# Transposing two blocks ahead, running half-array tiles in two groups, and loading w1 in two halves (RWKV-5 attention and sentence MoE)

## Chip, cores, metric

One core of one Trainium2 chip. The metric is device time in microseconds (us), lower is better. Runs come with the granted clock of TensorE. Ratios are the mean time of one kernel's fast runs over that of the other's fast runs of the same rounds, so they are not quite the ratio of the medians quoted beside them. A run is called slow when it took over 1.5% more than the fastest run of the same kernel; slow runs stay in the medians and ranges but out of the ratios. In traces PE is TensorE (PEld its weight loads), DVE VectorE, ACT ScalarE, POOL GpSimd.

## The reference

B = 4 sequences of S = 768 tokens, H = 8 heads of D = 48; F = 1024; 8 experts. First a linear attention with decay, then a mixture of experts that picks one expert per whole sequence:

```python
for t in range(S):                       # attention, per batch and head
    cur = (u * k_t) outer v_t
    y[t] = r_t @ (state + cur)
    state = w * state + k_t outer v_t
x = y as [B, S, H * D]
e = argmax(mean over S of x @ w_gate)    # one expert per sequence
out = gate_weight * (relu(x @ w1[e]) @ w2[e])
```

Note what the gate means for time: which expert's w1 and w2 a sequence needs is known only after its last token has been through the attention.

## The kernel before

A sequence is cut into 3 blocks of 256 tokens, 12 blocks g in all (N = 12, NB = 3). For block g: `transposes(g, c)` turn the scaled k and r (full 128*128 array), `scores` makes the masked products (`at`, then `gt` by VectorE; 64*64 tiles), `scores_v` makes the outputs y and the state s (64*128 tiles), `inter` adds the state's part (full array), `add_bonus` adds the u term (64*64), `backs` transposes y back and sums it for the gate. The prediction writes T(g, c) for `transposes(g, c)`, Y1 and Y0 for `scores_v(g, 1)` and `scores_v(g, 0)`, "at 0" and "at 1" for the two calls of `scores`. The MoE's matmuls of the sequence before are cut into jobs (16 `mm1` of three hp matmuls, which multiply by w1, and 12 `mm2` of four op matmuls, which multiply by w2, per sequence), and each `slot()` in the loop takes about RATE of them from a list:

```python
RATE = 8.5 / 7
def slot():
    if acc[1]:
        acc[0] += RATE
        c = int(acc[0])
        acc[0] -= c
        moe(c)                # up to c jobs, if so many are in the list
    else:
        fill(2, 256)          # idle matmuls on zeros
# ... cut ...
for g in range(NB, N):
    # ... cut: POOL scales k and r and casts v of block g + 2, next load ...
    transposes(g + 1, 0)
    slot()
    scores_v(g, 1, True)
    slot()
    transposes(g + 1, 1)
    if gi: inter(g, 0)
    scores_v(g, 0, gi == 0)
    add_bonus(g)
    evac_y(g, 0)
    slot()
    inter(g, 1)
    evac_y(g, 1)
    scores(g + 1, 0)
    slot()
    backs(g)
    if last: pool_sum(b)
    slot()
    acc[1] = True
    if last:
        gate(b)               # then the expert is known
        weights(b)            # POOL issues the DMAs of w1 and w2; 28 new jobs
    scores(g + 1, 1)
    slot()
    bonus(g + 1)
    if last: gate_weight(b)
    slot()
moe(len(jobs))
```

TensorE runs the program in this order. Before the loop, blocks 0 to 2 and gate 0 are written out by hand, with POOL's order there

```python
    gate(0)
    weights(0)
    prep_r(4)
    prep_v(4)
```

## Time and profile before

| | before |
|---|---|
| time, median of the 4 runs beside the changed kernel | 154.63 us (154.41 to 156.17) |
| profiled span | 152.6 us |
| PE busy | 139.5 us, 91% |
| granted clock, mean | 0.978 |
| PE waits for a weight DMA | none |

The lines that matter are in the prediction below. How to read them: the table by stretch shows TensorE busy nearly all the time from 41 us on, so what its stream contains is what the time is.

### The profile page before, as it was taken

How to read it: one execution, taken by the hardware profiler on the slowest of the kernel's cores; microseconds unless marked ns; L12 is line 12 of the kernel's file. 1: busy time of each engine (PE TensorE's matmuls, PEld its weight loads, DVE VectorE, ACT ScalarE, POOL GpSimd, SP SyncE). 2: the span in 40 equal slices, each digit the busy share in tenths (PEclk: the TensorE clock that was granted, in tenths of full speed). 3: DMA queues.
4: the chain of work that ended last, by engine and by line, in shares of the span. 5: the costliest groups of instructions: out<-in, count | busy, mean ns of one | idle time of the engine just before them, and what ended most of it. 6: DMA issues, size and time to landing. Idle time of an engine off the chain costs nothing.

```text
span 152.6 us, 4539 instructions
## 1 busy us (share of the span) xinstructions
PE 139.5 (91%) x1951; PEld 97.9 (64%) x1951; DVE 74.4 (49%) x164; ACT 83.6 (55%) x144; POOL 68.5 (45%) x62
## 2 busy tenths in 40 slices
PE   6999877956989999999999999999999999999991
PEld 2266645644767878766677877666777765676560
DVE  7837796125465654754548456465562321121110
ACT  0976567351356766546476784563664543556231
POOL 4169659207976839289292862963021020000000
PEclk9999999995599999999999999999999999999999
DMA  2999998303999999999991000998020079960034
GB/s 59 301 322 321 279 268 226 99 0 92 227 215 297 249 312 269 293 214 210 215 376 48 4 0 4 153 195 267 22 93 4 0 111 208 161 247 0 0 126 185
DMA packets 41464, 25.47 MB, mean 167 GB/s; under 512 B 38755, under 2 KB 39012, under 8 KB 41444
## 3 DMA queue, kind: packets, MB, share of 16 engines
q1 hardware_dynamic: 39460, 18.89, 42.9%
q0 software_dynamic: 1152, 6.29, 22.3%
q8 instruction: 15, 0.25, 0.6%
q10 hardware_dynamic: 832, 0.00, 0.3%
q14 instruction: 5, 0.04, 0.1%
HBM read 26.76 MB, written 4.72 MB: 206 GB/s over the span
## 4 chain that ended last, share of the span: by engine, by line
PE 78%; DVE 10%; ACT 8%; issue 2%; DVEq 0%
PE op L503 21%; PE hp L483 21%; PE twp L236 7%; PE at L260 5%; DVE gt L268 5%; PE fill L113 5%; PE y L353 5%; ACT kr L246 4%; PE s L361 2%; PE xp L402 2%; ACT ht L490 2%; PE y L313 2%; PE y L323 2%; DVE ht L492 1%; DVE st L376 1%
## 5 line engine op out<-in xcount | busy, mean ns | idle before, releaser
L483 PE MATMUL hp<-xt,w 128*128 128x384 bf16 x192 | 41.4, 334 | 1.3 <-DVE lg L436 0.3
L503 PE MATMUL op<-w,ht 128*128 128x384 bf16 x192 | 34.9, 326 | 0.1
L246 ACT COPY kr<-twp 128x1024 bf16<-128x1024 bf16 x24 | 24.1, 1011 | 18.4 <-PE twp L236 18.4
L268 DVE TENSOR_TENSOR gt<-at,mask 128x1024 bf16<-128x1024 f32 x24 | 29.3, 1221 | 8.8 <-PE at L260 8.6
L490 ACT ACTIVATE ht<-hp 128x384 bf16<-128x384 f32 x48 | 23.4, 491 | 17.8 <-PE hp L483 17.1
L483 PEld LDWEIGHTS <-w 128*128 128x128 bf16 x192 | 25.0, 148 | 8.1 <-issue 4.4
L305 POOL TENSOR_TENSOR vt<-vb,tcol 128x768 bf16<-128x768 bf16 x11 | 16.3, 1477 | 25.4 <-DVE tcol L297 25.4
L503 PEld LDWEIGHTS <-ht 128*128 128x128 bf16 x192 | 17.3, 97 | 11.1 <-issue 0.8
L247 DVE TENSOR_TENSOR prod<-twp,kr 128x512 bf16<-128x512 bf16 x24 | 10.2, 424 | 27.8 <-ACT kr L246 27.8
L199 POOL TENSOR_TENSOR kp<-k,dk 128x768 bf16<-128x768 f32 x11 | 20.0, 1816 | 1.4 <-DMA k<-in_k_dram 1.4
L199 POOL TENSOR_TENSOR rp<-r,dr 128x768 bf16<-128x768 f32 x11 | 20.0, 1820 | 0.0
L510 ACT ACTIVATE ob<-op,gw 128x384 f32<-128x384 f32 x16 | 9.3, 581 | 13.2 <-PE op L503 12.9
L113 PE MATMUL fill<-zero 128*128 128x512 bf16 (+1 forms) x45 | 14.5, 430 | 1.9 <-DVE zero L85 1.3
L353 PEld LDWEIGHTS <-gt 64*128 64x128 bf16 x384 | 11.5, 94 | 5.0 <-issue 3.9
L492 DVE TENSOR_SCALAR ht<-hp 128x384 bf16<-128x384 f32 x16 | 8.9, 554 | 11.7 <-PE hp L483 11.5
L353 PE MATMUL y<-vb,gt 64*128 64x48 bf16 x384 | 14.1, 182 | 0.4 <-ACT xn L389 0.4
L260 PE MATMUL at<-kr 48*64 48x128 bf16 x384 | 10.5, 229 | 3.6 <-ACT kr L246 1.7
L389 ACT CAST xn<-y 128x384 bf16<-128x384 f32 x24 | 11.1, 480 | 4.1 <-PE y L323 3.5
L462 POOL DMA_DIRECT2D w<-in_moe_w_dram x4 | 2.5, 623 | 22.5 <-DVE gw L452 7.8
L260 PEld LDWEIGHTS <-kr 48*64 48x64 bf16 x384 | 7.0, 110 | 8.2 <-issue 6.2
L410 ACT COPY xt<-xp 128x768 bf16<-128x768 bf16 x12 | 9.6, 798 | 4.3 <-PE xp L402 4.3
L361 PE MATMUL s<-vb,kp 64*128 64x96 bf16 x160 | 10.5, 208 | 0.4 <-DVE st L376 0.4
(73 smaller groups left out, 155.6 us busy)
## 6 DMA issues: line engine op xcount, KB each, us to landing
w<-in_moe_w_dram POOLq DMA_DIRECT2D x8, 768.0 KB, 10.2
k<-in_k_dram SPq DMA_DIRECT2D x12, 384.0 KB, 5.1
r<-in_r_dram SPq DMA_DIRECT2D x12, 384.0 KB, 5.8
v<-in_v_dram SPq DMA_DIRECT2D x12, 384.0 KB, 5.7
out_dram<-ob SPq DMA_DIRECT2D x11, 384.0 KB, 5.6
out_dram<-ob SPq DMA_DIRECT2D x2, 192.0 KB, 1.9
wuT<-in_w_dram ACTq DMA_DIRECT2D x2, 0.8 KB, 3.6
wuT<-in_u_dram ACTq DMA_DIRECT2D x2, 0.8 KB, 4.1
```

The lines of the kernel that those rows point to most:

```text
L113: nc.tensor.matmul(out=fills[-1][:, 0:cols], lhsT=zero[:, 0:128], rhs=zero[:, 0:cols], start=True, stop=True)
L199: eng.tensor_mul(dst[:, cs, :, 0:D].rearrange("q c h d -> q h c d"), src[:, :, cs, :], dec[:, :, cs, :])
L246: nc.scalar.copy(kts[g][:, :, :, c, :], tw)
L260: nc.tensor.matmul(out=at[64 * j : 64 * j + 64, a, pp, cs, :], lhsT=kt[q, p, j, cs, :], rhs=rt[q, p, j].rearrange("q c i -> q (c i)"), sta ...
L268: nc.vector.tensor_mul(gts[g][:, rnd].rearrange("q a p c t -> q (a p) c t"), at.rearrange("q a p c t -> q (a p) c t"), mask.rearrange("q n ...
L305: nc.gpsimd.tensor_mul(vt, vbs[g].rearrange("q c h d -> q (c h) d"), tcol.to_broadcast([128, 2 * H, D]))
L353: nc.tensor.matmul(out=yj[:, D * h : D * h + D], lhsT=gt[q, p // 2, a, p % 2, c, :], rhs=vb[q, c, h, :], start=(first and i == 0), stop=(c ...
L361: nc.tensor.matmul(out=sp[:, 96 * p : 96 * p + 96], lhsT=kp[g % NR][qo, c, 2 * p : 2 * p + 2, :].rearrange("s a b -> s (a b)"), rhs=vb[qo, ...
L389: nc.scalar.copy(xns[g][:, j, :], ys[g][j][:, 0:DM])
L483: nc.tensor.matmul(out=hp[:, 0:SB], lhsT=w1[:, ct, ft::NFT], rhs=xts[b][:, ct, SB * sb : SB * sb + SB], start=(ct == 0), stop=(ct == NCT - 1),
L490: nc.scalar.activation(out=o, in_=hp[:, 0:SB], func=ACT.Relu)
L503: nc.tensor.matmul(out=op[:, 0:DM], lhsT=ht[:, ft, 128 * si : 128 * si + 128], rhs=w2[:, ft, :], start=(ft == 0), stop=(ft == NFT - 1),)
```

## The change

Intent: each switch of TensorE between tilings costs time, and a block has four runs of half-array tiles. If the transposes are done two blocks ahead, block g + 1's scores can stand directly behind block g's outputs, in two runs. In the same go the block gets an eighth slot at the same RATE, jobs begin at the second slot of block 3, the gate's VectorE copy of the logits goes, and w1 comes in two DMAs of half the columns, so that the first jobs of a sequence need only the first. The diff, cut to its core (left out: prod split from transposes, helpers that let y be built in pieces, POOL's work in the loop, now for block g + 3 instead of g + 2, and w2's rows, arranged to match the halves of w1):

```diff
-        scores_v(g, 1, True)          # loop, cut and reordered for reading
-        slot()
-        if n1: transposes(g + 1, 1)
+        scores_v(g, 1)
+        if n1: scores(g + 1, 0)
+        slot()
+        if n2: transposes(g + 2, 0)
+        acc[1] = True
+        slot()
+        slot()
         if gi: inter(g, 0)
         scores_v(g, 0)
         add_bonus(g)
+        if n1: scores(g + 1, 1)
+        inter(g, 1)
         evac_y(g, 0)
+        evac_y(g, 1)
+        slot()
         slot()
-        inter(g, 1)
-        evac_y(g, 1)
-        if n1: scores(g + 1, 0)
-        slot()
         backs(g)                      # now sums for the gate first, then transposes
+        if n1: bonus(g + 1)
         slot()
         if last: gate(b); weights(b); gate_weight(b)
-        if n1: scores(g + 1, 1)
+        if n2: transposes(g + 2, 1)
         slot()
-        if n1: bonus(g + 1)
         slot()
```
```diff
-        w1 = wpool.tile([128, NCT, F], BF16, ...)
-        nc.gpsimd.dma_start(out=w1..., in_=moe_w1[ds(ev, 1)]...)
+        for fh in range(2):
+            t = wpool.tile([128, NCT, HF], BF16, ...)
+            nc.gpsimd.dma_start(out=t, in_=moe_w1[ds(ev, 1)]...[:, :, HF * fh : HF * fh + HF])
-                out=hp[:, 0:SB], lhsT=w1[:, ct, ft::NFT],
+                out=hp[:, 0:SB], lhsT=w1[ft // 4][:, ct, ft % 4 :: 4],
```
```diff
     scores(3, 1)                      # before the loop
     bonus(3)
+    prep_k(5); prep_r(5); prep_v(5); load(9)
+    transposes(4, 0); prod(4, 0)
+    fill(2, 256)
+    transposes(4, 1); prod(4, 1)
```

RATE itself is not in the diff: it stays 8.5/7.

More of the change, by code (lines that the diff above doesn't have):

```diff
@@ L70, with load @@
     raw = {}
-    def load(g):
+    def load(g, which="krv"):
         b, gi = divmod(g, NB)
         for name, src in (("k32", k), ("r32", r), ("v32", v)):
+            if name[0] not in which:
+                continue
             t = inp.tile([128, H, 2, D], FP32, tag=name, name=f"{name}_{g}")
@@ L195 @@
     vbs, kts, rts, prods, gts, vts, ys, sts, xns = {}, {}, {}, {}, {}, {}, {}, {}, {}
-    s_ps, xts, carry, tcols = {}, {}, {}, {}
+    s_ps, xts, carry, tcols, tws = {}, {}, {}, {}, {}
     def scale(eng, dst, src, dec, cs):
@@ L226, in prep_v, with transposes @@
         vbs[g] = vb
-    def transposes(g, c):
+    def transposes(g, c, eng=None):
         if c and g < NB + 2:
@@ L245, in transposes, with prod @@
         tw = twp.rearrange("q o (j i) -> q o j i", j=2)
-        nc.scalar.copy(kts[g][:, :, :, c, :], tw)
-        nc.vector.tensor_mul(prods[g][:, :, c], tw[:, 0:NP], rts[g][:, :, :, c, :])
+        if eng is nc.vector:
+            nc.vector.tensor_copy(kts[g][:, :, :, c, :], tw)
+        else:
+            nc.scalar.copy(kts[g][:, :, :, c, :], tw)
+        tws[g, c] = tw
+    def prod(g, c):
+        nc.vector.tensor_mul(prods[g][:, :, c], tws.pop((g, c))[:, 0:NP], rts[g][:, :, :, c, :])
     def scores(g, rnd):
@@ L307, in vt_mul, with begin, y_bank @@
         vts[g] = vt
+    begun = set()
+    def begin(g, j):
+        if (g, j) in begun:
+            return False
+        begun.add((g, j))
+        return True
+    def y_bank(g, j):
+        if g not in ys:
+            ys[g] = [
+                pp_y.tile([128, 512], FP32, tag=f"y{i}", name=f"y{i}_{g}") for i in range(2)]
+        return ys[g][j]
     def inter(g, j):
         st, rt = sts.pop((g, j)), rts[g]
-        yj = ys[g][j]
+        yj = y_bank(g, j)
         for p in range(NP):
@@ L315, in inter @@
                 lhsT=rt[:, p, j].rearrange("q c i -> q (c i)"), rhs=st[:, p, :],
-                start=(j == 0 and p == 0), stop=False, skip_group_check=True,
+                start=begin(g, j), stop=False, skip_group_check=True,
             )
@@ L326, in add_bonus, with y_mms, mm, state_mms @@
             )
-    def scores_v(g, j, first):
-        gi = g % NB
-        if j:
-            ys[g] = [
-                pp_y.tile([128, 512], FP32, tag=f"y{i}", name=f"y{i}_{g}") for i in range(2)]
-        gt, vb, yj = gts[g], vbs[g], ys[g][j]
-        o = 1 - j
-        with_state = not (o == 1 and gi == NB - 1)
+    def y_mms(g, j, heads=range(H)):
+        q = slice(64 * j, 64 * j + 64)
+        gt, vb, yj = gts[g], vbs[g], y_bank(g, j)
+        def mm(h, c):
+            p, a = divmod(h, 2)
+            nc.tensor.matmul(
+                out=yj[:, D * h : D * h + D],
+                lhsT=gt[q, p // 2, a, p % 2, c, :], rhs=vb[q, c, h, :],
+                start=begin(g, j), stop=(c == 1), skip_group_check=True,
+            )
+        return [lambda h=h, c=c: mm(h, c) for h in heads for c in range(2)]
+    def state_mms(g, o):
+        b, gi = divmod(g, NB)
+        if o == 1 and gi == NB - 1:
+            return []
         if o == 0:
-            b = g // NB
             if gi == 0:
@@ L346, in scores_v, with mm @@
                 )
-        sp = s_ps[g // NB]
-        q, qo = slice(64 * j, 64 * j + 64), slice(64 * o, 64 * o + 64)
-        def y_mm(i):
-            h, c = divmod(i, 2)
-            p, a = divmod(h, 2)
-            nc.tensor.matmul(
-                out=yj[:, D * h : D * h + D],
-                lhsT=gt[q, p // 2, a, p % 2, c, :], rhs=vb[q, c, h, :],
-                start=(first and i == 0), stop=(c == 1), skip_group_check=True,
-            )
-        def s_mm(i):
-            p, c = divmod(i, 2)
+        sp, vb = s_ps[b], vbs[g]
+        qo = slice(64 * o, 64 * o + 64)
+        def mm(p, c):
             nc.tensor.matmul(
@@ L364, in s_mm, with together, state_out @@
                 rhs=vb[qo, c, 2 * p : 2 * p + 2, :].rearrange("s a b -> s (a b)"),
-                start=(gi == 0 and o == 0 and i == 0), stop=(c == 1), skip_group_check=True,
-            )
-        for i in range(H):
-            y_mm(2 * i)
-            if with_state:
-                s_mm(i)
-            y_mm(2 * i + 1)
-        if not with_state:
+                start=(gi == 0 and o == 0 and p == 0 and c == 0), stop=(c == 1),
+                skip_group_check=True,
+            )
+        return [lambda p=p, c=c: mm(p, c) for p in range(NP) for c in range(2)]
+    def together(ymm, smm):
+        for i in range(max(len(ymm), 2 * len(smm))):
+            if i < len(ymm):
+                ymm[i]()
+            if i % 2 == 0 and i // 2 < len(smm):
+                smm[i // 2]()
+    def state_out(g, o):
+        b, gi = divmod(g, NB)
+        if o == 1 and gi == NB - 1:
             return
@@ L376, in scores_v @@
         nc.vector.tensor_mul(
-            st, sp[:, 0 : 2 * D * NP].rearrange("q (p e) -> q p e", p=NP),
+            st, s_ps[b][:, 0 : 2 * D * NP].rearrange("q (p e) -> q p e", p=NP),
             wcmask if o else bmask.rearrange("q p a d -> q p (a d)"),
@@ L380, in scores_v @@
         if o:
-            carry[g // NB] = st
+            carry[b] = st
             sts[g + 1, 0] = st
@@ L384, in scores_v, with evac_y, pool_mms, turn_back @@
             sts[g, 1] = st
-    def evac_y(g, j):
-        if j == 0:
-            xns[g] = work.tile([128, 2, DM], BF16, tag="xn", name=f"xn{g}")
-        nc.scalar.copy(xns[g][:, j, :], ys[g][j][:, 0:DM])
-    def backs(g):
+    def scores_v(g, j):
+        smm = state_mms(g, 1 - j)
+        together(y_mms(g, j), smm)
+        state_out(g, 1 - j)
+    def evac_y(g, j, eng=None):
+        if g not in xns:
+            xns[g] = work.tile([128, 2, DM], BF16, tag="xn", name=f"xn{g}")
+        if eng is nc.vector:
+            nc.vector.tensor_copy(xns[g][:, j, :], ys[g][j][:, 0:DM])
+        else:
+            nc.scalar.copy(xns[g][:, j, :], ys[g][j][:, 0:DM])
+    def pool_mms(g):
+        gi = g % NB
+        for j in range(2):
+            for ct in range(NCT):
+                o = DM + 2 * NB * ct + 2 * gi + j
+                nc.tensor.matmul(
+                    out=s_ps[g // NB][:, o : o + 1], lhsT=xns[g][:, j, ct::NCT], rhs=ones_col,
+                    start=False, stop=True, skip_group_check=True,
+                )
+    def turn_back(g):
         b, gi = divmod(g, NB)
@@ L394, in backs @@
             xts[b] = xpool.tile([128, NCT, S], BF16, tag="xt", name=f"xt{b}")
-        xn, sp = xns.pop(g), s_ps[b]
+        xn = xns.pop(g)
         xp = pp_tw.tile([128, 2 * NP, 128], BF16, tag="tw", name=f"xp{g}")
@@ L402, in backs @@
                 nc.tensor.transpose(out=xv[:, ct, :, j, :], in_=xn[:, j, ct::NCT], identity=ident)
-        for j in range(2):
-            for ct in range(NCT):
-                o = DM + 2 * NB * ct + 2 * gi + j
-                nc.tensor.matmul(
-                    out=sp[:, o : o + 1], lhsT=xn[:, j, ct::NCT], rhs=ones_col,
-                    start=False, stop=True, skip_group_check=True,
-                )
         nc.scalar.copy(xts[b][:, :, L * gi : L * gi + L], xp)
@@ L412, in backs @@
             d.pop(g, None)
+    def backs(g):
+        pool_mms(g)
+        turn_back(g)
     gates, gws = {}, {}
@@ L434, in gate @@
             )
-        lg = gpool.tile([128, E], FP32, tag="lg", name=f"lg{b}")
-        nc.vector.tensor_copy(lg, lgp[:, 0:E])
+        lg = lgp[:, 0:E]
         top8 = gpool.tile([128, 8], FP32, tag="top8", name=f"top8{b}")
@@ L456 @@
     jobs = []
+    HF = F // 2
     def weights(b):
@@ L460, in weights @@
         ev = nc.gpsimd.value_load(idx8[0:1, 0:1], min_val=0, max_val=E - 1)
-        w1 = wpool.tile([128, NCT, F], BF16, tag="w1", name=f"w1_{b}")
-        nc.gpsimd.dma_start(
-            out=w1.rearrange("p ct f -> p (ct f)"),
-            in_=moe_w1[ds(ev, 1)].rearrange("o (p ct) f -> p (o ct f)", ct=NCT))
+        w1 = []
+        for fh in range(2):
+            t = wpool.tile([128, NCT, HF], BF16, tag=f"w1_{fh}", name=f"w1_{b}_{fh}")
+            nc.gpsimd.dma_start(
+                out=t,
+                in_=moe_w1[ds(ev, 1)].rearrange("o (p ct) f -> p (o ct) f", ct=NCT)[
+                    :, :, HF * fh : HF * fh + HF])
+            w1.append(t)
         w2 = wpool.tile([128, NFT, DM], BF16, tag="w2", name=f"w2_{b}")
         nc.gpsimd.dma_start(
-            out=w2.rearrange("p ft m -> p (ft m)"),
-            in_=moe_w2[ds(ev, 1)].rearrange("o (p ft) m -> p (o ft m)", ft=NFT))
+            out=w2.rearrange("p (fh ft) m -> p fh (ft m)", fh=2),
+            in_=moe_w2[ds(ev, 1)].rearrange("o (fh p ft) m -> p (o fh) (ft m)", fh=2, p=128))
         ht = hpool.tile([128, NFT, S], BF16, tag="ht", name=f"ht{b}")
@@ L545, in outputs @@
             inter(g, 0)
-        scores_v(g, 0, g % NB == 0)
+        scores_v(g, 0)
         add_bonus(g)
@@ L561 @@
     transposes(0, 0)
+    prod(0, 0)
     transposes(0, 1)
+    prod(0, 1)
     fill(4, 512)
@@ L574 @@
     transposes(1, 0)
+    prod(1, 0)
     transposes(1, 1)
-    scores_v(0, 1, True)
+    prod(1, 1)
+    scores_v(0, 1)
     prep_v(1)
@@ L580 @@
     scores(1, 0)
-    scores_v(0, 0, True)
+    scores_v(0, 0)
     transposes(2, 0)
+    prod(2, 0)
     fill(1, 512)
@@ L587 @@
     transposes(2, 1)
+    prod(2, 1)
     prep_v(2)
@@ L594 @@
     scores(2, 0)
-    scores_v(1, 1, True)
+    scores_v(1, 1)
     backs(0)
@@ L598 @@
     inter(1, 0)
-    scores_v(1, 0, False)
+    scores_v(1, 0)
     scores(2, 1)
@@ L610 @@
     gap()
-    scores_v(2, 1, True)
+    scores_v(2, 1)
     outputs(2, [gap] * 3)
@@ L614 @@
     transposes(3, 0)
+    prod(3, 0)
     gate(0)
@@ L625 @@
     transposes(3, 1)
+    prod(3, 1)
     fill(2, 256)
@@ L630 @@
     bonus(3)
+    prep_k(5)
+    prep_r(5)
+    prep_v(5)
+    load(9)
+    transposes(4, 0)
+    prod(4, 0)
+    fill(2, 256)
+    transposes(4, 1)
+    prod(4, 1)
     for g in range(NB, N):
@@ L634 @@
         last = gi == NB - 1
-        n1, n2 = g + 1 < N, g + 2 < N
-        if n2:
-            prep(g + 2)
-            prep_v(g + 2)
-            if g + 2 + AHEAD < N:
-                load(g + 2 + AHEAD)
-        if n1:
-            transposes(g + 1, 0)
+        n1, n2, n3 = g + 1 < N, g + 2 < N, g + 3 < N
+        if n3:
+            prep(g + 3)
+            prep_v(g + 3)
+            if g + 3 + AHEAD < N:
+                load(g + 3 + AHEAD)
+        scores_v(g, 1)
+        if n1:
+            scores(g + 1, 0)
+        slot()
+        if n2:
+            transposes(g + 2, 0)
+            prod(g + 2, 0)
+        acc[1] = True
         slot()
-        scores_v(g, 1, True)
         slot()
-        if n1:
-            transposes(g + 1, 1)
         if gi:
             inter(g, 0)
-        scores_v(g, 0, gi == 0)
+        scores_v(g, 0)
         add_bonus(g)
+        if n1:
+            scores(g + 1, 1)
+        inter(g, 1)
         evac_y(g, 0)
+        evac_y(g, 1)
         slot()
-        inter(g, 1)
-        evac_y(g, 1)
-        if n1:
-            scores(g + 1, 0)
         slot()
@@ L661 @@
             pool_sum(b)
+        if n1:
+            bonus(g + 1)
         slot()
-        acc[1] = True
         if last:
@@ L666 @@
             weights(b)
-        if n1:
-            scores(g + 1, 1)
+            gate_weight(b)
+        if n2:
+            transposes(g + 2, 1)
+            prod(g + 2, 1)
         slot()
-        if n1:
-            bonus(g + 1)
-        if last:
-            gate_weight(b)
         slot()
```

## The prediction

> **What bounds the kernel now.** I read, in order, the busy shares, the 40 slices, the chain, a table by stretch, and the timeline of TensorE.
>
> ```profile
> PE 139.5 (91%) x1951; PEld 97.9 (64%) x1951; DVE 74.4 (49%) x164; ACT 83.6 (55%) x144; POOL 68.5 (45%) x62
> ...
> PE   6999877956989999999999999999999999999991
> ...
> PEclk9999999995599999999999999999999999999999
> ...
> PE 78%; DVE 10%; ACT 8%; issue 2%; DVEq 0%
> ```
> ```profile
> 41.30:115.00 73.70, 72.58 (x1205) 54.24 (x1204) 41.79 (x82) 45.59 (x78) 43.53 (x33) 1.00 0.72 180
> 131.00:152.60 21.60, 17.74 (x99) 11.60 (x96) 3.47 (x6) 8.78 (x17) 0.00 (x0) 1.00 0.36 121
> ```
> The columns of the table are length, busy time of PE, PEld, DVE, ACT, POOL, granted clock, DMA share, GB/s. From 41.3 us on, PE is busy 72.58 of 73.70 us at full clock, and no other engine is busy over 62% of it. So in the loop over blocks the order and the content of TensorE's stream are the time. A gain has to shorten that stream; a wait put into it adds in full.
>
> What it holds besides useful work shows in the starts of one block:
>
> ```profile
> 66.23 0.81 PE L503 MATMUL op<-w,ht 128*128 128x384 bf16 x4
> 66.98 0.19 PE L353 MATMUL y<-vb,gt 64*128 64x48 bf16 x1
> ...
> 67.30 0.26 PE L353 MATMUL y<-vb,gt 64*128 64x48 bf16 x4
> 67.48 0.82 PE L503 MATMUL op<-w,ht 128*128 128x384 bf16 x4
> ...
> 69.00 0.25 PE L353 MATMUL y<-vb,gt 64*128 64x48 bf16 x4
> 69.19 0.36 PE L323 MATMUL y<-vt,ident 64*64 64x384 bf16 x4
> 69.48 1.47 PE L503 MATMUL op<-w,ht 128*128 128x384 bf16 x8
> 70.79 0.33 PE L313 MATMUL y<-st,kr 128*128 128x96 bf16 x4
> 71.05 0.42 PE L260 MATMUL at<-kr 48*64 48x128 bf16 x16
> 71.40 0.82 PE L503 MATMUL op<-w,ht 128*128 128x384 bf16 x4
> ```
> In an unbroken row, op matmuls start 0.163 us apart (48 of them in 7.82 us in the chain). Four take 0.65, but 0.75 (66.23 to 66.98) when half-array tiles follow: 0.10 to enter. Four y matmuls, 0.025 apart, take 0.10, but 0.18 or 0.19 before op or before the 64*64 L323: 0.08 to leave, and as much from 64*128 to 64*64. L323 streams 0.17 and takes 0.29: 0.12 to leave. L313 takes 0.26 before L260 for four of 0.0425: 0.09 to enter. Where L260 is followed by L323 early in the program (24.02 to 24.26) it takes 0.25, not 0.35: 0.10 to leave, and next to nothing between two 64*64 groups.
>
> The last part is about the experts' weights, which can only be fetched once a sequence's gate is known:
>
> ```profile
> 119.30 0.78 PE L431 MATMUL lgp<-wg,pooled 128*128 128x8 f32 x6
> ...
> 120.59 0.16 DVE L440 FIND_INDEX8 idx<-top,lg 128x8 uint32<-128x8 f32 x1
> ...
> 122.05 0.59 POOL L462 DMA_DIRECT2D w<-in_moe_w_dram  x1 [6.96 <-PE hp L483]
> ```
> ```profile
> DMA to landing us min/median/max: 6.4/7.3/9.0
> ```
> From the gate's first matmul to the issue is 2.75 us, to the landing of w1 (the view of the lines that load it, L462) 9.2 at best. The chain shows what covers it now: 6 + 3 hp and 48 op of the sequence before, until 131.2; w1 landed near 128.5. No PE wait there.
>
> **What the Trainium skill says.** "TensorEngine Tiling (Array Packing)", Key Properties: changing the tiling mode drains TensorE. The trace agrees: 0.08 to 0.12 us at each change, both ways. "SBUF — State Buffer", the note on cachelines: 16 bytes, with full bandwidth from two hits to a line. The w1 columns are 8 bf16 apart now (16 bytes) and 4 (8 bytes) after; LDWEIGHTS of w1 takes 148 ns and of ht, with neighbouring columns, 97; of xn, 6 bytes apart, 104. So this agrees for stride. "TensorE: Matmul & The Clock Gate", Part 1: an idle window of some 3.4 us halves the clock. The trace agrees: PEclk is 5 in two slices after the thin stretch 31 to 35 us (PE 2.07 busy of 4.00, clock 0.50 from 34.5 to 41.3, 6.8 us). "DMA: Bandwidth & Descriptors", Issuing engines are not separate DMA queues: all issues share the same 16 engines; the 9.0 us landing is the one issued while r and v loads were in flight, the 6.4 us ones had few beside them.
>
> **Part 1, the runs of half-array tiles.** Before, a block has the runs Y1; Y0 + L323; at 0; at 1. After: Y1 + at 0; Y0 + L323 + at 1. First merge: out goes an exit of 0.08 and an entry of 0.09, in comes one change 64*128 to 64*64 of 0.08: saves 0.09 to 0.10. Second merge: L323's exit 0.12 and the entry 0.09 go, some 0.04 may stay: saves 0.17. Three fewer first matmuls after a change, each late by 0.01 (op) or 0.06 (hp: 0.22 to its successor instead of 0.16), mean 0.035: 0.10. Sum 0.37 us a block, 8 blocks have scores: **-3.0 us**.
>
> **Part 2, w1's stride.** In a row, hp runs 0.162 apart already, so the slow load is hidden. It shows only in the first hp after a change or after very short matmuls, about 25 times by the starts in the trace, 0.045 each: **-1.2 us** (little of it counted above).
>
> **Part 3, the slots.** The rate per slot stays 8.5/7, but a block has 8 slots instead of 7, and the first block starts filling at slot 2 instead of 6. Counting both programs: before, 16, 42 and 67 MoE jobs are done when gates 1, 2 and 3 are computed; after, 25, 54 and 83 of 28, 56 and 84 that exist. So only 3, 2 and 1 jobs are left to cover the new w1. PE between a gate and the first matmul on that w1: gate 0.74, transposes 0.45, then jobs of 0.65 and pieces of attention:
> - gate 1: two jobs, Y1 + at 0 (1.0), a job: 4.1 us.
> - gate 2: two jobs: 2.5.
> - gate 3: no transposes, one job: 1.4.
>
> The weights: the lg copy is gone (0.2), so issue at 2.55. Half of w1 is 0.39 M elements. w2, as large as w1 and queued behind it, lands 5.7 us after it (11.5 + 0.63 - 6.4), so half takes 2.85; the start costs 6.4 - 5.7 = 0.7, by the first packets rather 1.2: estimate 4.0 from issue. Landing 6.5 after the gate. Waits: 2.4, 4.0 and 5.1: **+11.5 us**. Without the halves it would be 2.4 more for each. The second half and w2 land before they are used (8 jobs, 4 to 5 us later).
>
> **Part 4, the clock.** Waits of 4 and 5 us are longer than a 3.4 us window; I expect half clock after the last two and perhaps the first, each losing 1 to 1.7 us of progress: **+3 us**.
>
> **Part 5, the ends.** Start: in block 3, T(5,0) stands second, and needs POOL's rp for block 5, which ended at 44.2 and comes 0.6 later for the added weight DMA; before, PE had done Y0, L323, inter, at 1 and backs (1.9 us) by 45.0, after it has not: **+1.9**. Tail: w1 jobs at the end run 0.63 us each (16 in 10.1: two PSUM banks, evacuation) against 0.49 in the loop; five fewer run so: **-0.6**.
>
> Sum: 154.7 - 3.0 - 1.2 + 11.5 + 3 + 1.9 - 0.6 = 166.3. I chose **166.0 us**.
>
> **Rivals.**
> 1. The waits don't appear because the slots are slower than I count, and the changed order with shorter runs wins: 154.7 - 3.0 - 1.2 - 0.6 = 149.9 to 152. For it: someone who halved w1 was looking at just this arrival. Against: the stream is in order, the counts are arithmetic, and nothing else stands between gate 3 and its w1.
> 2. The halves land much earlier (2 us from issue): waits 0.4, 2.0, 3.1, no cold clock: 154.7 - 4.8 + 5.5 + 1.9 = 157.3, just within 2%. Against: no weight landing here was under 6.4.
> 3. The short runs of 2 KB instead of 12 KB in w1 make POOL's issue and the transfer slower (each half as long as w1 now, 6.4), and the clock falls three times: 11.5 + 7 + 5, some 173.
> 4. ACT or DVE becomes the bound in bursts (two evacuations of y together, kr copies late in the block): ACT has 28 us free of 73.7 in the loop, so at most tenths of a us a block.
>
> **Range and chances.** Parts 1 and 2 are safe to 1 us, Part 3 to 3, Part 4 to 3, the start to 1.5. The range 160 to 171 holds most of that. Slower by over 2% means over 157.8, which fails only if rival 1 or 2 holds: 0.91; within 2%: 0.07; faster: 0.02.
>
> **What would show it.** PE idle of some 2.4, 4 and 5 us ahead of hp with the w1 DMA as releaser, at blocks 6, 8 and 11; slices with PEclk 5 late in the span; L260 directly behind L353 and L323 with no 0.09 between; LDWEIGHTS of w1 near 105 ns; one op job only between the last gate and hp. I am wrong if hp of a new sequence starts without a wait, or if the clock stays full.

## The result

182.16 us median (180.42 to 183.1, 4 runs), against 154.63 us: ratio 1.174, interval 1.162 to 1.187. Slower, as predicted, but by 27.5 us instead of 11.3, outside the range. The page of the changed kernel, with the lines that answer to the first fence of the prediction:

```profile
PE 147.0 (81%) x1945; PEld 97.9 (54%) x1945; DVE 75.3 (42%) x160; ACT 84.3 (47%) x144; POOL 73.4 (40%) x66
...
PE   7998679777699999981998999509899993199992
...
PEclk9999955555559999998799999966999998559998
...
PE 61%; DMA 10%; ACT 10%; POOL 6%; DVE 6%; issue 4%; POOLq 1%; DVEq 0%; ACTq 0%
```

DMA has come into the chain with 10%. There are holes in PE at three places (1, 5 0, 3 1 in the digits), and the clock is at half from the sixth slice to the twelfth and again behind the second and the third hole. The view of waits names the holes (who waited for what: us in total, times, longest):

```profile
PE hp L535 <- DMA w<-in_moe_w_dram: 18.1, 3, 7.0
```

The timeline of the changed kernel at the third gate shows how one arises (start, length, engine, line):

```profile
149.63 0.73 PE L478 MATMUL lgp<-wg,pooled 128*128 128x8 f32 x6
150.21 0.81 PE L555 MATMUL op<-w,ht 128*128 128x384 bf16 x4
...
150.68 0.17 DVE L486 FIND_INDEX8 idx<-top,lgp 128x8 uint32<-128x8 f32 x1
...
152.08 1.57 POOL L512 DMA_DIRECT2D w<-in_moe_w_dram  x2 [10.06 <-DVE gw L498]
...
158.06 1.14 PE L535 MATMUL hp<-xt,w 128*128 128x384 bf16 x3 [7.04 <-DMA w<-in_moe_w_dram]
```

One op job is left after the gate, then PE stands still for 7.04 us. The expert's number is known at 150.85, POOL issues at 152.08, and the first half of w1 is there at 158.0, 8.4 us after the gate's first matmul.

The intended part is there too. In the same kernel L268 (scores) stands directly behind L346 (the bonus), both in 64*64 tiles (the view shows 48*64, as D is 48), and L346 now takes 0.19 us to its successor where L323 took 0.29 before:

```profile
72.33 0.28 PE L358 MATMUL y<-vb,gt 64*128 64x48 bf16 x5
72.54 0.36 PE L346 MATMUL y<-vt,ident 64*64 64x384 bf16 x4
72.73 0.40 PE L268 MATMUL at<-kr 48*64 48x128 bf16 x16
73.06 0.34 PE L336 MATMUL y<-st,kr 128*128 128x96 bf16 x4
```

And the start has become long. From the first pooling sums of block 0 to those of block 3 the table by stretch gives 20.68 us before and 31.87 after (columns as in the prediction; the tenth is the clock):

```profile
22.98:43.66 20.68, 16.24 (x316) 11.99 (x316) 9.45 (x22) 9.61 (x15) 12.89 (x10) 0.83 0.58 136
```
```profile
22.81:54.68 31.87, 25.58 (x348) 18.61 (x348) 12.57 (x24) 11.93 (x18) 19.17 (x15) 0.52 0.66 147
```

Of these 11.2 us, work that before came later makes up 2.8: one transpose group more (0.45 us), one scores group more (0.35), and four jobs (4 times 0.49). So 8.4 us are lost there, net of four idle matmuls fewer (13 for 17). In that stretch PE waits for POOL twice, which has three weight DMAs to issue first (38.87 to 41.3; before, two in 1.25 us) and then scales r of blocks 4 and 5 one after the other:

```profile
43.20 0.61 PE L238 MATMUL twp<-ident,rp 128*128 128x128 bf16 x4 [1.28 <-POOL rp L201]
...
48.92 0.61 PE L238 MATMUL twp<-ident,rp 128*128 128x128 bf16 x4 [1.12 <-POOL rp L201]
```

So three suspects for 27.5 us: the waits (18.1), what the clock loses behind them, and the start. The experiments take them one by one.

### The profile page after: what moved, and what is told of

Read it like the earlier page. It is cut to its first block, busy times and chain, and to the rows that moved or that the text cites. A ratio compares the mean times of both kernels' runs of the same rounds, so it can differ in the third digit from the quotient of the medians.

```text
span 181.3 us, 4525 instructions
## 1 busy us (share of the span) xinstructions
PE 147.0 (81%) x1945; PEld 97.9 (54%) x1945; DVE 75.3 (42%) x160; ACT 84.3 (47%) x144; POOL 73.4 (40%) x66
## 3 DMA queue, kind: packets, MB, share of 16 engines
q0 software_dynamic: 4288, 6.29, 20.8%
## 4 chain that ended last, share of the span: by engine, by line
PE 61%; DMA 10%; ACT 10%; POOL 6%; DVE 6%; issue 4%; POOLq 1%; DVEq 0%; ACTq 0%
PE hp L535 19%; PE op L555 15%; DMA w<-in_moe_w_dram 10%; PE twp L238 5%; ACT kr L251 4%; PE y L358 4%; PE at L268 3%; PE fill L115 3%; ACT ht L542 3%; DVE gt L276 3%; PE y L336 2%; POOL vt L313 2%; PE s L384 2%; PE xp L452 2%; PE y L346 2%
## 5 line engine op out<-in xcount | busy, mean ns | idle before, releaser
L535 PE MATMUL hp<-xt,w 128*128 128x384 bf16 x192 | 43.5, 363 | 19.9 <-DMA w<-in_moe_w_dram 18.1
L535 PEld LDWEIGHTS <-w 128*128 128x128 bf16 x192 | 21.1, 120 | 33.6 <-DMA w<-in_moe_w_dram 19.2
L555 PE MATMUL op<-w,ht 128*128 128x384 bf16 x192 | 34.3, 326 | 0.1
L255 DVE TENSOR_TENSOR prod<-twp,kr 128x512 bf16<-128x512 bf16 x24 | 10.2, 424 | 30.3 <-ACT kr L251 30.3
L512 POOL DMA_DIRECT2D w<-in_moe_w_dram x8 | 6.4, 804 | 23.9 <-DVE gw L498 23.9
L358 PEld LDWEIGHTS <-gt 64*128 64x128 bf16 x384 | 12.6, 98 | 6.4 <-issue 5.4
L429 ACT CAST xn<-y 128x384 bf16<-128x384 f32 x24 | 11.2, 479 | 10.3 <-PE y L346 9.7
L358 PE MATMUL y<-vb,gt 64*128 64x48 bf16 x384 | 15.3, 188 | 0.4 <-ACT xn L429 0.4
L115 PE MATMUL fill<-zero 128*128 128x512 bf16 (+1 forms) x39 | 13.7, 463 | 1.5 <-DVE zero L87 1.3
L268 PE MATMUL at<-kr 48*64 48x128 bf16 x384 | 11.2, 241 | 2.5 <-ACT kr L251 1.1
L238 PE MATMUL twp<-ident,rp 128*128 128x128 bf16 x96 | 11.2, 250 | 2.4 <-POOL rp L201 2.4
L238 PE MATMUL twp<-ident,kp 128*128 128x128 bf16 x96 | 11.2, 251 | 1.2 <-ACT xt L453 1.2
```

The lines of the kernel that those rows point to most:

```text
L115: nc.tensor.matmul(out=fills[-1][:, 0:cols], lhsT=zero[:, 0:128], rhs=zero[:, 0:cols], start=True, stop=True)
L238: nc.tensor.transpose(out=twp[:, o + p, :], in_=src[:, c, 2 * p : 2 * p + 2, :].rearrange("s a b -> s (a b)"), identity=ident,)
L268: nc.tensor.matmul(out=at[64 * j : 64 * j + 64, a, pp, cs, :], lhsT=kt[q, p, j, cs, :], rhs=rt[q, p, j].rearrange("q c i -> q (c i)"), sta ...
L358: nc.tensor.matmul(out=yj[:, D * h : D * h + D], lhsT=gt[q, p // 2, a, p % 2, c, :], rhs=vb[q, c, h, :], start=begin(g, j), stop=(c == 1), ...
L429: nc.scalar.copy(xns[g][:, j, :], ys[g][j][:, 0:DM])
L535: nc.tensor.matmul(out=hp[:, 0:SB], lhsT=w1[ft // 4][:, ct, ft % 4 :: 4], rhs=xts[b][:, ct, SB * sb : SB * sb + SB], start=(ct == 0), stop ...
```

## Experiments

Theory: the eighth slot at an unchanged RATE makes the jobs of the old sequence run out before the new sequence's w1 has landed; PE, being in order, stops, and the clock falls. Rival: the new order is itself slower (late transposes, two evacuations at once, start).

### 1. Pacing, both ways round

`a1_rate`: the changed kernel, paced as before.

```diff
-    RATE = 8.5 / 7
+    RATE = 8.5 / 8
-        acc[1] = True      # after the first slot of the loop
+        acc[1] = True      # after the sixth
```

> The changed kernel with its whole order kept, but the MoE jobs paced as before: 8.5 jobs a block (rate 8.5/8) and starting at the seventh slot of block 3, so that 17, 42 and 68 jobs are done at the gates instead of 25, 54 and 83. Theory (the jobs run ahead of the weights): the three waits of PE for the w1 DMA, 18.1 us together, vanish, and with them the cold windows behind them; only the cold start may stay. Time 152 to 160 us, and if the clock stays full at the start, 150 to 153. Rival (the new order itself is at fault: late transposes, evacuations in bursts, start): it stays above 165.

`b1_ahead`: the kernel before, paced as the changed one.

```diff
-    RATE = 8.5 / 7
+    RATE = 8.5 / 7 * 8 / 7
-        acc[1] = True      # after the fifth slot
+        acc[1] = True      # after the first
```

> The kernel before with its order kept, but MoE jobs paced as in the changed kernel: rate 8.5/7*8/7, from the second slot of block 3, so 24, 54 and 83 jobs are done at the gates. w1 is whole. Theory: PE waits for the w1 DMA at each new sequence, some 4.5, 6.5 and 7 us, plus cold windows: 172 to 180 us. Rival (the order is at fault): it stays within 3% of before, 154 to 159.

Measured: `a1_rate` 160.69 us (159.44 to 161.22), ratio 1.042, just above the 152 to 160 that I expected; PE waits for no weight DMA and the clock is full from 52 us to the end. `b1_ahead` 182.22 us median; its two fast runs are 180.29 and 180.65 (two slow ones, 183.8 and 184.3, are left aside, so there is no interval), just above my 172 to 180. The old order with the new pacing thus comes to the same time as the changed kernel, by longer waits and without the long start:

```profile
PE hp L483 <- DMA w<-in_moe_w_dram: 23.9, 4, 8.3
```

Four waits here, as w1 is whole and jobs start before even sequence 0's w1 is there. The theory holds: pacing alone makes some 26 us in one kernel and takes some 21 from the other. But a1_rate stays 6 us behind the kernel before, more than I wanted to see, so the rival has a part as well. Where: not in the loop. Over six whole blocks (pooling sums of block 4 to those of block 10) with the same 51 jobs, the first line is the kernel before, the second `a1_rate`:

```profile
52.88:110.91 58.03, 57.68 (x940) 42.76 (x938) 32.67 (x68) 35.58 (x61) 32.68 (x25) 1.00 0.70 174
```
```profile
60.64:116.34 55.70, 54.90 (x931) 39.73 (x929) 31.91 (x64) 35.44 (x60) 30.81 (x24) 1.00 0.72 164
```

2.33 us less; one transpose group less falls in this stretch (0.45), so 1.88, or 0.31 us a block. That is the gain that the change was made for. The six us are lost in the start: 28.96 us from the first pooling sums to the fourth, where before took 20.68.

### 2. The halves of w1

`b2_halves`: the kernel before with w1 in halves and w2's rows arranged to match, nothing else. `a2_whole`: the changed kernel with w1 whole.

```diff
-        w1 = wpool.tile([128, NCT, F], ...); one dma_start     # b2_halves; a2_whole is the reverse
+        two tiles of [128, NCT, HF], one dma_start each
-        lhsT=w1[:, ct, ft::NFT]
+        lhsT=w1[ft // 4][:, ct, ft % 4 :: 4]
```

> The kernel before with w1 in two halves (columns 4 apart instead of 8) and w2 arranged to match, nothing else. Theory: LDWEIGHTS of w1 falls from 148 to about 120 ns as in the changed kernel, of use only in the first hp matmul after a change of tiling, so -0.5 to -1.2 us: 153.5 to 154.5 us. Rival (the third weight DMA on POOL delays prep and the start): 155 to 157.

> The changed kernel with w1 whole again (columns 8 apart) and w2 as before. In the changed kernel the first half landed 6.1 to 6.5 us after its issue, hardly before a whole w1 in the kernel before (6.4 at best), with both halves' packets in flight together. Theory A (halves share the engines and gain almost nothing): 180 to 185 us, the waits within 0.7 us of the changed kernel's. Theory B (as predicted, a half saves over 2 us a wait): 188 to 192.

Measured: `b2_halves` 156.57 us (155.49 to 157.93), ratio 1.015 (1.003 to 1.027): the rival of that run, not my theory. LDWEIGHTS of w1 does fall from 148 ns in the mean to 116, but over the six blocks it gives 57.80 us for 58.03, 0.04 a block; and the start is 2.1 us longer (22.77 for 20.68), with PE waiting 1.3 us for r of block 4 behind the third weight DMA on POOL. `a2_whole` 182.71 us, ratio 1.186 beside 1.174: about the scatter of the changed kernel. The view of the lines that load w1 gives landing times, minimum, median and maximum, first for the changed kernel (both halves of four sequences), then for `a2_whole` (whole w1):

```profile
DMA to landing us min/median/max: 5.9/6.8/9.4
```
```profile
DMA to landing us min/median/max: 6.8/7.2/8.4
```

By the trace the first halves of sequences 1 to 3 took 6.1, 6.5 and 5.9 us, whole ones in the same places 6.8, 7.2 and 7.2. Half the bytes come only 0.6 to 1.3 us earlier, and the waits are 18.1 us with halves and 20.7 without. What is won there goes again in the start: from the first pooling sums to the fourth, `a2_whole` takes 28.13 us for the same work that takes 31.87 with three weight DMAs. So the halves are worth about nothing here, which settles the size of that step: I had put 2.4 us a wait on it.

Why a half takes so long was tried with `a4_delay`: five memsets on POOL, 2.88 us, between the issues of the two halves.

```diff
             w1.append(t)
+            if b and fh == 0:
+                for _ in range(5):
+                    nc.gpsimd.memset(scratch, 0.0)
```

> The changed kernel with five memsets on POOL (some 3 us) between the DMA of the first half of w1 and that of the second, for sequences 1 to 3. Theory A (the halves share the 16 engines): with the second half 3 us behind, the first lands 4.0 to 4.8 us after its issue instead of 5.9 to 6.5, the waits shrink by 1.3 to 2 us each, time down by 4 to 6 us. Theory B (short packets and start-up alone set it): landing still about 6 us and the time unchanged within 1 us.

Measured: 179.42 us (179.01 to 181.39), ratio 1.158 beside 1.174. First halves of sequences 1 to 3 now land after 5.0, 6.4 and 5.2 us, so 1.1, 0.1 and 0.7 earlier; waits 16.1 us instead of 18.1. Both theories missed: sharing the engines with the second half is at most part of it, and a lone half still takes 5 us or more. (In `a1_rate` the first halves of sequences 2 and 3, with the second half right behind them but no load or store in flight beside them, took 5.5 and 5.4 us, hardly longer than that.) The packets may be the rest: the page of the changed kernel counts 4288 packets on the weight queue for the 6.29 MB that came in 1152 before, and POOL spends 0.80 us on each half's issue where the whole w1 took 0.59. That is not separated further and stays open, as does why sequence 2 hardly moved.

### 3. The clock behind the waits

`a3_fill`: idle matmuls on zeros where PE waits anyhow.

```diff
     def mm1(b, w1, ht, ft, sb):
+        if b and ft == 0 and sb == 0:
+            fill_bank()
+            fill((0, 20, 29, 31)[b], 512)
```

> The changed kernel with idle matmuls on zeros (20, 29 and 31 of 512 columns, 4.3, 6.3 and 6.7 us) put ahead of the first hp of sequences 1, 2 and 3, where PE waits for w1 anyhow. The waits stay. Theory (the half clock behind each wait is a cost of its own, 1.4 + 1.9 + 1.8 us by comparing blocks): granted clock full from the start of the loop on, time down by 4 to 6 us, 176 to 179 us. Rival (the clock costs nothing there, or doesn't answer to such fills): 181 to 184.

Measured: 177.04 us median; two fast runs, 174.34 and 176.34 (two slow ones, no interval). The waits are nearly as long, now filled with zeros (each first hp still starts 0.04 or 0.05 us after its w1 has landed), and the clock stays up behind them. `a3_fill` in the slices:

```profile
PEclk9999996555569999999999999999999999999999
```

The same stretches with the same work, wait included: blocks 5 to 6 take 15.86 us in the changed kernel and 14.48 here, blocks 8 to 9 18.84 and 16.95, and from the first hp of sequence 3 to the end 23.26 and 21.47. Sum of the differences: 5.1 us. Of these 0.5 us are not the clock: in the first two stretches hp starts 0.12 and 0.38 us sooner after the gate, as w1 happened to land sooner. So the halved clock behind the waits costs about 4.6 us of its own, 1.3, 1.5 and 1.8. (The median of all runs falls by 5.1 us; that of the fast ones by more, but their start was faster too, 30.09 us for 31.87 in the profiled runs.)

### 4. The start

Two causes are at hand: POOL's order (after gate 0 it issues three weight DMAs and only then scales blocks 4 and 5, though it sat idle for 11.5 us ahead of their issue, 7.8 in the kernel before), and `backs`, which now sums for the gate before it transposes back and so waits for both halves of y and, in block 1, for VectorE. `d1_backs` undoes the second in `a1_rate`; `c1_early` undoes both:

```diff
 # d1_backs and c1_early, blocks 0 to 2 only
-        pool_mms(g)
-        turn_back(g)
+        turn_back(g)     # transposes, then the pooling sums, then the copy
 # c1_early only
+    prep_r(4); prep_v(4); prep_k(5); prep_r(5); prep_v(5)
     gate(0)
     weights(0)
-    prep_r(4); prep_v(4)
     ...
-    prep_k(5); prep_r(5); prep_v(5)
```

> a1_rate with only one of c1_early's two mends: in blocks 0 to 2 the transposes back come before the pooling sums, as in the kernel before; POOL's order stays as in the changed kernel. Splits the 6.3 us between a1_rate (160.7) and c1_early (154.4). If POOL (added weight DMA, and scaled k and r of blocks 4 and 5 needed earlier) is the larger part: 158.5 to 160 us, with PE still idle some 1.2 us before the transposes of r of blocks 4 and 5. If the order of pooling is: 155 to 157.

> a1_rate (pacing as before) with the start mended in two ways: POOL scales k, r and v of blocks 4 and 5 before it waits for gate 0 instead of after (it sits idle 7.8 us there in the kernel before), and in blocks 0 to 2 the transposes back come before the pooling sums again. Theory (a1_rate is 6 us behind before only by its start, some 7.5 us, while its loop is 0.3 us a block faster): time 150 to 153.5 us, faster than the kernel before. Rival (the start is slow for the half clock or the added transposes, not for POOL): 157 to 161.

`b3_early` moves POOL's work in the same way in the kernel before.

> The kernel before with POOL's work for blocks 4 and 5 ahead of gate 0, nothing else. It tells how much of c1_early's gain is the new order's and how much this move gives by itself: in the kernel before PE waits about 0.5 us for rp of block 4, so 152.5 to 154.5 us is expected; if the move is worth more than 2 us here too, the start of both kernels hangs on POOL.

Measured: `a1_rate` 160.69, `d1_backs` 158.07 (157.17 to 159.36, ratio 1.021), `c1_early` 154.42 us (153.93 to 155.88, ratio 0.995). By these medians 2.6 us hang on the order of the pooling sums and 3.7 on POOL; the profiled runs (160.16, 158.85 and 155.88 us) give 1.3 and 3.0. So the split is good to a us or so; POOL's is the larger part either way. In `c1_early` POOL works through the 8 us ahead of the gate instead of idling:

```profile
27.36 1.81 POOL L201 TENSOR_TENSOR rp<-r,dr 128x768 bf16<-128x768 f32 x1
29.11 0.83 POOL L227 CAST vb<-v 128x768 bf16<-128x768 f32 x1
29.89 1.82 POOL L201 TENSOR_TENSOR kp<-k,dk 128x768 bf16<-128x768 f32 x1
31.67 1.80 POOL L201 TENSOR_TENSOR rp<-r,dr 128x768 bf16<-128x768 f32 x1
...
36.54 1.71 POOL L518 DMA_DIRECT2D w<-in_moe_w_dram  x2 [2.31 <-DVE gw L504]
```

and PE no longer waits for r. `b3_early`: 155.16 us, ratio 1.000 (0.990 to 1.011): in the old order the move is worth nothing, where I had expected up to 2 us. (The old order transposes block 5 only later; that this is the reason was not tested.) `c1_early` fell short of my 150 to 153.5: at equal pacing it ties with the kernel before, because its start is still some 2 to 4 us longer (25.07 us from the first pooling sums to the fourth against 20.68, of which 0.8 is work done early, and its profiled run had the half clock there for 20.5 us, the kernel before for 6.8). How much the clock may be worth there shows `b3_early`: its profiled run, of 156.31 us, has the old order and the half clock for 20.5 us too, and takes 23.00 us in that stretch, 2.3 more than the kernel before.

### 5. A version that keeps the gain

`c2_jobs` puts jobs in the place of idle matmuls in block 3, `c3_warm` adds idle matmuls in PE's waits of blocks 0 and 1, `c4_paced` leaves more jobs for the first gate:

```diff
 # c2_jobs, over c1_early
-    RATE = 8.5 / 8                      # from the seventh slot of block 3
+    RATE = 8.2 / 8                      # from the second
 # c3_warm, over c2_jobs
+    fill(2, 512)                        # before scores(2, 0) and before scores_v(1, 1)
+            fill((1, 4, 1)[g], 512)     # before the pooling sums of blocks 0 to 2
 # c4_paced, over c3_warm
-    RATE = 8.2 / 8
+    rate = [7.0 / 8]                    # 8.9 / 8 after gate 1
```

> c1_early with MoE jobs instead of idle matmuls from the second slot of block 3 on, at rate 8.2/8, so that 21, 46 and 70 jobs are done at the gates (7, 10 and 14 left to cover the fetch). Saves the idle matmuls of five slots (1.2 us): 152.5 to 154 us. If the cover is too thin, waits for the w1 DMA come back at sequences 1 to 3 and it is slower than c1_early.

> c2_jobs with idle matmuls where PE waits in blocks 0 and 1 (before the scores of block 2, before Y of block 1, before the pooling sums). Runs of every kernel, of the one before as well, come in two kinds, 154.0 to 154.7 at a granted clock of 0.955 and more and 156.0 to 156.6 at 0.93 to 0.945, where the clock falls at 23 us already. If thin work[...] is the cause, the low kind vanishes and the time is 151.5 to 153.5 in all runs. If not, the spread stays and the median is that of c2_jobs or up to 1 us more.

> c3_warm with the MoE jobs slower until gate 1 (rate 7/8) and faster after (8.9/8): 18, 45 and 71 jobs done at the gates, 10, 11 and 13 left. In c3_warm's profiled run sequence 1's first half of w1 landed 10.4 us after its issue, with k, r and v loads in flight, and PE waited 3.8 us and then lost clock. Theory (pacing must leave enough jobs to cover the slowest landing): no wait for the w1 DMA at any sequence, all runs within 1 us of each other, 151 to 152.7 us, 1.5 to 2.5% faster than the kernel before. If waits remain or the spread of 152.5 to 157 stays, pacing isn't all of it.

Measured: `c2_jobs` 153.77 us (151.54 to 158.59), ratio of fast runs 0.988; `c3_warm` 153.61 (152.51 to 156.88), 0.989; both scatter, and three runs of each are slow. In `c2_jobs` the wait is back once, 2.7 us, at sequence 1, whose first half of w1 landed 9.3 us after its issue, with k, r and v loads in flight; in `c3_warm` 10.4 us. `c3_warm`'s eight runs all have a granted clock of 0.963 or more, where `c2_jobs` has 0.919 to 0.931 in three of seven, so the fills did keep the early clock up, but by themselves they moved the median by nothing. `c4_paced`: **152.72 us (152.12 to 153.05, six runs), ratio 0.987 (0.982 to 0.991)**, no PE wait for a weight DMA, and the scatter is gone. It was not the pacing alone: in the profiled runs PE has 6.6 us of work behind the issue at sequence 1 in `c2_jobs` and `c3_warm` and 9.1 in `c4_paced`, but the half also landed sooner there, after 7.6 us; one of 10.4 would still have cost a wait. 1.3% better than the kernel before: clear of noise, yet below 2%, and a little less than the 1.5 to 2.5% that I had expected.

## Why the prediction was wrong

The mechanism was right: jobs run ahead, PE waits for w1 at three gates, the clock falls, and the rest can't make up for it. The chance of slower, 0.91, was on the right side. Its sizes were off, all to the same side, two of them by some 6.5 us each:

| term of the sum | predicted | measured | shown by |
|---|---|---|---|
| runs of half-array tiles | -3.0 (0.37 a block) | 0.27 to 0.31 a block, some -2.3 | six blocks, a1_rate and b2_halves |
| w1's stride | -1.2 | 0.04 a block, some -0.3 | b2_halves |
| waits for w1 | +11.5 | +18.1 | waits; a1_rate, b1_ahead |
| half clock behind them | +3 | +4.6 | a3_fill |
| start | +1.9 | +8.4 | stretch; d1_backs, c1_early |
| tail | -0.6 | 0 | from the first hp of sequence 3 to the end 21.47 us, before and in a3_fill |

The measured terms sum to 154.7 - 2.3 - 0.3 + 18.1 + 4.6 + 8.4 = 183.2; the profiled run took 183.1. The tail's gain was a misreading: in both kernels the tail holds the 28 jobs of sequence 3 and no others, so there were no five to take out of it.

**The step that failed in the waits** (6.6 us too few) is "estimate 4.0 from issue" for half of w1. The cover was right: I had 4.1, 2.5 and 1.4 us of PE work after the gates, and in the trace the waits begin 4.1, 2.5 and 1.4 us after them. The issue was right too, 2.55 us after the gate, measured 2.5. But a half lands 5.9 to 6.5 us after its issue, nearly as late as a whole w1. I had taken the time between the landings of w1 and w2 as the time that a w1 takes, cut it in two, and so had treated a DMA's time as proportional to its bytes with nothing else in flight, although the second half is issued 0.8 us behind the first. Rival 3 of the prediction had this (a half as long as a w1, and three falls of the clock), but I left it outside my range; its terms also sum to 175.3, not 173. (Two slips more, from which nothing was worked out: half of w1 is called 0.39 M elements, which is all of it, and the cover in the kernel before is not 6 + 3 hp, the pieces on the chain alone, but 15 hp, and 48 op.)

**The step that failed in the start** (6.5 us too few) is a reading: I looked for the one dependency I had found (r of block 5, 0.6 us later) and took the rest of the written-out start as it stood. What the runs show is the third weight DMA (2.1 us by b2_halves, 3.7 by a2_whole), the moved pooling sums (1.3 to 2.6 by d1_backs) and POOL's order (3.0 to 3.7 between d1_backs and c1_early); these overlap, and the time at half clock differs between the profiles as well (10.2 us in b2_halves, 6.8 before). They stand in a stretch that has no slack: there the chain goes through ACT, DVE and POOL by turns, not through a full PE. The half clock in it (0.52 there in the profiled run, 0.83 before) may follow in part from the gaps, which no run tests; how much of the 8.4 us is clock and how much waiting was not separated (b3_early's 2.3 us more, with 20.5 us of half clock instead of 6.8, are the only hint).

**The clock** was the right mechanism, and 1.3 to 1.8 us each fits the 1 to 1.7 of the prediction; there were three falls, where it was sure of two. What it called agreement with the skill was less: the fall that it read in the kernel before came with no PE gap over 1.38 us and PE busy for 2.07 of the 3.41 us ahead, so not after an idle window; and I did not ask whether the thin start could fall earlier and stay down for 30.7 us, as it did.

**The tiles**: the second merge gave what was worked out (0.10 for L346's exit, and the entry); the 0.31 of a1_rate is lower than 0.37 by about what PE waits more in its six blocks (0.76 us for 0.35, or 0.07 a block). The stride was counted as 0.045 us saved at each of 25 late first matmuls. From a first hp to its successor the traces have 0.204 us before and 0.179 in b2_halves (means of 39), so some 1.0 us in all, yet its six blocks are only 0.23 us shorter; PE waits 0.22 us more there, and where the rest went was not found.

## What to carry to other kernels

Where independent work covers a fetch that is only known late, count the work left at the moment of the request against the slowest landing in the trace, not the fastest, and check that count again whenever the number of slots changes, even if the line with the rate isn't touched. Halving a DMA did not halve its landing time here: 5.9 to 6.5 us for 6.8 to 7.2 with the other half right behind it, and still 5.0 to 6.4 with it 3.7 us behind. And a gain of tenths of a us a block in a full loop is easily lost in the start, where another engine sets the pace: read that stretch by its own chain.

## What the Trainium skill lacked or had wrong

- "TensorEngine Tiling (Array Packing)", Key Properties: it says that a change of mode drains TensorE, without a figure. Here each change costs 0.08 to 0.12 us, 64*128 to 64*64 as much as to the full array; 64*64 behind 64*64 saves 0.10 (L323 to its successor 0.29 us before, L346 0.19 after).
- "SBUF — State Buffer", note on cachelines: two hits to a line of 16 bytes are said to give full bandwidth. Columns 8 bytes apart load faster than 16 apart (median 113 ns for 144), but not as fast as neighbours (98); and in a row hp matmuls start 0.162 us apart with either.
- "DMA: Bandwidth & Descriptors", fit for SWDGE (2.0 us and bytes over 436 GB/s): for half of w1 (384 KB written, twice that read) it gives, as an estimate, 2.9 to 3.8 us; alone on POOL's queue it took 5.0 to 6.4 (a4_delay), with its other half behind it 5.9 to 6.5 in the changed kernel and 5.4 at best (a1_rate). The page gives no time for a casting DMA.
- "TensorE: Matmul & The Clock Gate", Part 1: agrees for PE gaps of 4.5, 6.5 and 7.0 us, which halved the clock each time (dense matmuls on zeros in the gap prevented it, a3_fill). But the cold state is said to come after an idle window of some 3.4 us, and here PE needn't be idle so long: the clock halved after 3.41 us with PE busy for 2.07 and no gap over 1.38 (the kernel before), for 1.87 (the changed kernel, at 23.4 us), and after a gap of 2.69 us (c2_jobs).
- The same page has the warm-up of a kernel vary from run to run; it gives no figure for what a thinly filled stretch some 20 us into a kernel does. Here the kernel before has runs of 154 us at a clock of 0.97 and of 156.5 at 0.934.
